# The general path as loops with sums in SBUF, and the branch's flag ahead of the last copies

## The chip, the core and the metric

The kernel runs on one core of one Trainium2 chip. The metric is the time of one execution on the device, in microseconds (us). Engines: PE (TensorE), DVE (VectorE), ACT (ScalarE), POOL (GpSimd) and SP (SyncE); PEld is PE's weight load.

## The reference

A gated linear recurrence, whose output is the input of a feed-forward block:

```python
f = 1.0 / (1.0 + np.exp(-f_logit))
for t in range(S):
    state = f[:, :, t, :, None] * state + np.einsum('bhd,bhe->bhde', k[:, :, t], v[:, :, t])
    y[:, :, t] = np.einsum('bhd,bhde->bhe', q[:, :, t], state)
...
h = x @ w_in
sp = np.where(h > 20.0, h, np.log1p(np.exp(np.minimum(h, 20.0))))
g = h * np.tanh(sp)
return (g @ w_out).astype(np.float32)
```

Batch 4, 8 heads, 768 positions, head size 48; `x` is the recurrence's output as 3072 rows of 384, `w_in` is 384 x 2048 and `w_out` 2048 x 384, all float32.

## The kernel before

The kernel holds two ways to the result and a branch between them.

**The planned path** (lines 240 to 617) does the recurrence in chunks of 128 positions, 24 chunks in all, in a form that divides by running products of `f`, and the feed-forward block in 6 groups of 512 tokens by 16 tiles of d_ff, 96 units in all. A unit is nine matmuls of 128x512 into `h` (`moe_in`, line 212), nine steps of the activation on ACT, DVE and POOL (`mish`, lines 222 to 230), and nine matmuls into the three output banks `o` (`moe_out`, line 235). The activation's two output parts go to PE two units later (`LAG` = 2).

Nothing is issued as it is written. Every step goes to a `Plan` with its engine, an assumed cost and the names that it reads and writes (`add`, line 52). `Plan.order` (line 122) packs all steps forward and backward some fifty times on assumed costs and keeps the packing that ends first; `issue` (line 137) then emits each engine's instructions in that order. So each engine runs a fixed list, and waits between engines are semaphores.

Of the last unit of a group (`out_unit`, line 551), each of the three output tiles m = 0, 1, 2 has a PE step of three matmuls, a copy from PSUM to `ob` (DVE for m = 0 and 2 on line 581, ACT for m = 1 on line 578), and a transfer to `out` that SP issues (line 582).

**The flag.** The planned path's form is good only while the running products stay above a bound. `ends` holds each chunk's last product. Four steps after the loop over units (lines 607 to 613) compare them with the bound on DVE (line 608), add them up per partition on DVE (line 611), over the partitions with a matmul against ones on PE (line 612), and copy the count to `flag` on DVE (line 613).

**The branch.** Line 621 loads `flag` into a register of each engine, and line 622 is a branch of each engine. With this reference's inputs all products are good, so every engine jumps over the body of the branch, the **general path** (lines 623 to 696), which is in the program and doesn't run. Behind the body, each engine brings its semaphores to the counts that the body would have left, and these stand in the trace under line 622. SP has eight of them, for its transfers' semaphores. Then come the waits and the barrier that close the program, under line 758.

The general path is a scan over time per head pair (a loop over batches, the four head pairs written out, a loop over the 48 columns of v for each pair), and then the feed-forward block for a group of 512 tokens at a time (a loop over the six groups, with the 24 gathers of its input and the 16 d_ff tiles written out). So it has six loops in its code. As compiled, the body that the branch jumps over has these numbers of instructions: PE 740, SP 381, ACT 278, DVE 244, POOL 169. SP's 381 are 55 transfers with about 105 instructions for their addresses, and for the rest the loops' scaffolding (branches, barriers, semaphores).

Of the kernel before, what the change touches and what calls it, by code (L numbers as in the profile page):

```python
# [160 lines left out]
def T_DVE(n):  # L161
    return n / 0.96 + 70
# [7 lines left out]
def recurrence_moe_kernel(  # L170
# [34 lines left out]
    state0 = ctile([P, P], F32, "state0")  # L205


    def moe_in(h, xt, j):
        n = 0
        for a in range(NK):  # L210
            for w, x in ((wih, 0), (wih, 1), (wil, 0)):
                nc.tensor.matmul(  # L212
                    h, w[:, j, a * P : (a + 1) * P], xt[:, x, a, :], start=(n == 0), stop=(n == 3 * NK - 1)
                )
                n += 1
# [14 lines left out]
            ("pool", T_POOL(GT), 1, lambda: nc.gpsimd.tensor_tensor(gl, g, gh.bitcast(F32), ALU.subtract)),  # L230
        )

    def moe_out(o, m, gh, gl, j, first, last):
        for i, (w, x) in enumerate(((woh, gh), (wol, gh), (woh, gl))):
            nc.tensor.matmul(  # L235
                o, w[:, j, m * P : (m + 1) * P], x, start=(first and i == 0), stop=(last and i == 2)
            )


    with tc.tile_pool(name="work", bufs=1) as pool, tc.tile_pool(  # L240
# [307 lines left out]
        while done < 4 * GC:  # L548
            attend()

        def out_unit(u):
            g, j = units[u]
            half = g < 2
            first = j == 0 or (half and j == HF)
            last = j == NF - 1 or (half and j == HF - 1)
            part = half and j == NF - 1
            gs = u % 3
            if part:
                for m in range(NK):
                    add("sp", 500, lambda m=m, g=g: nc.sync.dma_start(ob_[m], halves[g][m * P : (m + 1) * P, :]),  # L560
                        [("half", g, m)], pairs(("ob", m)), 262)
            if u == 0:
                plan.until = len(plan.steps)
            if last or first:
                for m in range(NK):
                    add("pe", 702, lambda m=m: moe_out(o_[m], m, gh_[gs], gl_[gs], j, first, last),
                        [("w", "h", j), ("w", "l", j), ("gh", gs), ("gl", gs)], [("o", m)])
            else:
                add("pe", 2106, lambda: [moe_out(o_[m], m, gh_[gs], gl_[gs], j, first, last) for m in range(NK)],
                    [("w", "h", j), ("w", "l", j), ("gh", gs), ("gl", gs)], [("o", m) for m in range(NK)])  # L570
            if last:
                dst = halves[g] if j < NF - 1 else out[:, g * GT : (g + 1) * GT]
                for m in range(NK):
                    if part:
                        add("dve", T_DVE(GT), lambda m=m: nc.vector.tensor_tensor(ob_[m], o_[m], ob_[m], ALU.add),
                            [("o", m)], pairs(("ob", m)))
                    elif m == 1:
                        add("act", T_ACT(GT, True), lambda m=m: nc.scalar.activation(ob_[m], o_[m], AF.Copy),  # L578
                            [("o", m)], pairs(("ob", m)))
                    else:  # L580
                        add("dve", T_DVE(GT), lambda m=m: nc.vector.tensor_copy(ob_[m], o_[m]), [("o", m)], pairs(("ob", m)))
                    add("sp", 500, lambda m=m, dst=dst: nc.sync.dma_start(dst[m * P : (m + 1) * P, :], ob_[m]),
                        pairs(("ob", m)), [("half", g, m) if half else ("out", g, m)], 262)

        for u in range(len(units) + LAG):
            if u < len(units):
                g, j = units[u]
                if g == 0:
                    split_w(j)
                x, hs, us, gs = g % 2, u % 2, u % 2, u % 3  # L590
                xk = [(hl, ("xt", x, c), p) for hl in "hl" for c in range(GC) for p in range(NK)]
                h = h_[hs]
                add("pe", 2106, lambda h=h, x=x, j=j: moe_in(h, xt_[x], j), xk + [("w", "h", j), ("w", "l", j)], [("h", hs)])
                kh, kn, kg = ("h", hs), ("n", us), ("g", us)
                ops = mish(h, n_[us], g_[us], gh_[gs], gl_[gs])
                rw = (
                    ([kh], [kn]), ([], [kn]), ([], [kn]), ([kh, kn], [kg]), ([kn], [kh]), ([], [kh]),
                    ([kh], [kg]), ([kg], [("gh", gs)]), ([kg, ("gh", gs)], [("gl", gs)]),
                )
                for (e, c, shared, fn), (r, w) in zip(ops, rw):  # L600
                    add(e, c, fn, r, w, port=shared)
            while done < min(4 * NCH, attend_goal(u)):
                attend()
            if u >= LAG:
                out_unit(u - LAG)

        ok, oks = at1[0:1, 0:1], state.rearrange("p b a c -> p (b a c)")[:, : NCH * NP]
        add("dve", 119, lambda: nc.vector.tensor_scalar(
            oks, ends.rearrange("p n a b -> p (n a b)"), -DEC_OK, None, ALU.is_le),
            [x for n in range(NCH) for x in pairs(("end", n))], [("st", b) for b in range(B)])  # L610
        add("dve", 169, lambda: nc.vector.tensor_reduce(okc, oks, mybir.AxisListType.X, ALU.add), [("st", 0)], ["okc"])
        add("pe", 26, lambda: nc.tensor.matmul(ok, ones, okc, start=True, stop=True), ["okc"], [("at", 2)])
        add("dve", 65, lambda: nc.vector.tensor_copy(flag, ok), [("at", 2)], ["flag"])

        plan.idle = idle
        with tc.manual_schedule():
# [3 lines left out]
    total = P * NCH * NP  # L620
    good = nc.values_load(flag[0:1, 0:1], min_val=0, max_val=total)
    with tc.If(good < total):
        xs = dram.tile([DM, NT], F32, tag="xs", name="xs")
        with tc.tile_pool(name="slow", bufs=1) as pool, tc.tile_pool(
            name="slow_psum", bufs=1, space=PSUM
# [6 lines left out]
            nc.gpsimd.memset(sel[0:64, 0:1], 1.0)  # L632
            nc.gpsimd.memset(sel[64:128, 1:2], 1.0)
            with tc.For_i(0, B, 1) as b:
                for p in range(NP):
                    f, k, q = (st([P, NCB, C], nm) for nm in ("sf", "sk", "sq"))
                    for dst, src in ((f, fl), (k, kk), (q, qq)):
                        nc.sync.dma_start(
                            dst, src.rearrange("(c b) p a t -> p a c b t", b=B)[:, p, :, ds(b, 1), :]
                            .rearrange("p c b t -> p c (b t)"),  # L640
                        )
                    nc.scalar.activation(f, f, AF.Sigmoid)
                    f2, k2, q2 = (x.rearrange("p c t -> p (c t)") for x in (f, k, q))
                    with tc.For_i(0, D, 1) as e:
                        v = st([P, S], "sv")
                        for i in range(2):
                            nc.sync.dma_start(
                                v[64 * i : 64 * i + 64, :],
                                vt[ds(b, 1), 2 * p + i, ds(e, 1), :]
                                .rearrange("a c t -> (a c) t")  # L650
                                .broadcast_to([64, S]),
                            )
                        nc.vector.tensor_tensor(v, v, k2, ALU.mult)
# [8 lines left out]
                            nc.scalar.activation(y[:, s], ps, AF.Copy)  # L662
                        for i in range(2):
                            nc.sync.dma_start(
                                xs.rearrange("d (c b t) -> d c b t", b=B, t=C)[ds(e + (2 * p + i) * D, 1), :, ds(b, 1), :]
                                .rearrange("d c b t -> d (c b) t"),
                                y[i : i + 1, :].rearrange("d (c t) -> d c t", c=NCB),
                            )

            with tc.For_i(0, NG, 1) as g:  # L670
                x = st([P, NK, GT], "sx")
                tok = ds(g * GT, GT)
                for a in range(NK):
                    for e in range(2):
                        r, hd = 64 * e, head_at(a, e)
                        for m in range(3):
                            nc.sync.dma_start(
                                x[r + m : r + 64 : 4, a, :], xs[hd * D + m : (hd + 1) * D : 3, tok]
                            )
                        r0 = head_at(NP - 1, e) * D  # L680
                        nc.sync.dma_start(x[r + 3 : r + 64 : 4, a, :], xs[r0 + a : r0 + D : 3, tok])
                xt = pool.tile([P, 2, NK, GT], F32R, tag="sxt", name="sxt")
                nc.scalar.activation(xt[:, 0], x, AF.Copy)
                nc.vector.tensor_tensor(xt[:, 1], x, xt[:, 0].bitcast(F32), ALU.subtract)
                h, *o = (psum.tile([P, GT], F32, tag=f"so{m}", name=f"so{m}") for m in range(NK + 1))
                n, g = (st([P, GT], nm) for nm in ("sn", "sg"))
                gh, gl = (pool.tile([P, GT], F32R, tag=nm, name=nm) for nm in ("sgh", "sgl"))
                for j in range(NF):
                    moe_in(h, xt, j)
                    for *_, step in mish(h, n, g, gh, gl):  # L690
                        step()
                    for m in range(NK):
                        moe_out(o[m], m, gh, gl, j, j == 0, j == NF - 1)
                for m in range(NK):
                    nc.vector.tensor_copy(g, o[m])
                    nc.sync.dma_start(out[m * P : (m + 1) * P, tok], g)


_SHAPES = [
# [63 lines left out]
```

## Time and profile before

| what | us |
|---|---|
| median of three runs (534.45 to 538.31) | 536.96 |
| the profiled execution, its own time | 537.24 |
| its span, from the first to the last instruction | 535.5 |
| outside the span (537.24 less 535.5) | 1.7 |

The profile shows busy times of engines; instructions that only wait, branch, load a register or issue a transfer belong to an engine's sequencer, are marked with a q behind the engine's name, and are not busy time.

### The profile page before, as it was taken

The numbers are of one execution on the slowest core, as the hardware profiler recorded it, in microseconds if no ns is written. First come the engines' busy times: TensorE is split into PE (matmuls) and PEld (weight loads), VectorE is DVE, ScalarE is ACT, GpSimd is POOL, SyncE is SP. The second block draws the span as 40 slices with busy tenths as digits, with TensorE's granted clock in tenths as the row PEclk, the third lists the DMA queues.
The fourth block names the chain that finished last, engine by engine and source line by source line (L and its number), as shares of the span: only waits on it lengthen the run. The fifth ranks groups of instructions, "written<-read, shape, count | busy, mean of one in ns | idle before, by whom it ended". The sixth has DMA issues, their size and how long they took to land.

```text
span 535.5 us, 13156 instructions
## 1 busy us (share of the span) xinstructions
PE 512.4 (96%) x5362; PEld 408.3 (76%) x5362; DVE 382.8 (71%) x617; ACT 415.5 (78%) x746; POOL 174.2 (33%) x153
## 2 busy tenths in 40 slices
PE   7899989899998999999999999999999999999992
PEld 7787767677777777787877777787787778788881
DVE  5988999999996878785767577747565763645441
ACT  7767877799878878878887878878788776777770
POOL 2311332233234434333443333333241322132330
PEclk9999999999999999999999999999999999999997
DMA  7876444424520443231213232202221000100001
GB/s 232 283 242 234 147 138 144 151 87 156 169 74 2 140 139 110 65 115 41 61 40 109 59 102 80 60 21 89 66 94 41 2 1 31 38 21 2 1 1 66
DMA packets 23926, 48.92 MB, mean 91 GB/s; under 512 B 2800, under 2 KB 6256, under 8 KB 23856
## 3 DMA queue, kind: packets, MB, share of 16 engines
q1 hardware_dynamic: 23856, 47.98, 28.1%
q8 instruction: 44, 0.72, 0.5%
q14 instruction: 26, 0.21, 0.1%
HBM read 39.32 MB, written 6.29 MB: 85 GB/s over the span
## 4 chain that ended last, share of the span: by engine, by line
PE 68%; DVE 16%; ACT 6%; DMA 4%; issue 4%; SPq 0%; DVEq 0%; ACTq 0%
PE h L212 31%; PE o L235 29%; DVE n L224 3%; DMA l<-fl 2%; DVE g L225 2%; DVE g L228 2%; PE at L427 2%; DVE wl L324 2%; PE at L462 2%; PE at L474 2%; DVE wt L319 2%; PE at L385 1%; DVE wt L321 1%; DMA xt<-xt 1%; PE at L410 1%
## 5 line engine op out<-in xcount | busy, mean ns | idle before, releaser
L230 POOL TENSOR_TENSOR gl<-g,gh 128x512 fp32r<-128x512 f32 x96 | 128.3, 1337 | 265.9 <-ACT gh L229 247.6
L212 PE MATMUL h<-xt,wh 128*128 128x512 f32 x576 | 185.2, 402 | 8.4 <-DVE g L228 5.3
L212 PEld LDWEIGHTS h<-xt,wh 128*128 128x128 f32 x576 | 104.6, 188 | 37.0 <-DVE g L228 9.2
L235 PE MATMUL o<-gh,wh 128*128 128x512 f32 x288 | 116.0, 403 | 0.0
L212 PE MATMUL h<-xt,wl 128*128 128x512 f32 x288 | 114.1, 396 | 0.1
L235 PE MATMUL o<-gl,wh 128*128 128x512 f32 x288 | 114.1, 396 | 0.0
L235 PE MATMUL o<-gh,wl 128*128 128x512 f32 x288 | 113.3, 393 | 0.0
L224 DVE SCALAR_TENSOR_TENSOR n<-n 128x512 f32<-128x512 f32 x96 | 70.7, 737 | 57.6 <-ACT n L223 57.5
L228 DVE TENSOR_TENSOR g<-g,h 128x512 f32<-128x512 f32 x96 | 65.2, 681 | 40.1 <-ACT h L227 39.7
L222 ACT ACTIVATE n<-h,hcap 128x512 f32<-128x512 f32 x96 | 65.7, 685 | 34.1 <-PE h L212 33.5
L226 ACT ACTIVATE h<-n,two 128x512 f32<-128x512 f32 x96 | 66.0, 688 | 22.7 <-DVE g L225 22.6
L229 ACT ACTIVATE gh<-g 128x512 fp32r<-128x512 f32 x96 | 60.3, 628 | 24.4 <-DVE g L228 22.2
L225 DVE TENSOR_TENSOR g<-h,n 128x512 f32<-128x512 f32 x96 | 66.0, 687 | 7.3 <-POOL gl L230 1.1
L223 ACT ACTIVATE n<-n,hcap 128x512 f32<-128x512 f32 x96 | 69.1, 720 | 2.0
L235 PEld LDWEIGHTS o<-gl,wh 128*128 128x128 f32 x288 | 54.1, 188 | 13.7 <-POOL gl L230 0.6
L212 PEld LDWEIGHTS h<-xt,wl 128*128 128x128 f32 x288 | 54.1, 188 | 13.7 <-DVE wl L324 0.5
L235 PEld LDWEIGHTS o<-gh,wh 128*128 128x128 f32 x288 | 54.1, 188 | 12.8 <-ACT ob L578 0.3
L235 PEld LDWEIGHTS o<-gh,wl 128*128 128x128 f32 x288 | 54.1, 188 | 12.4
L227 ACT ACTIVATE h<-h 128x512 f32<-128x512 f32 x96 | 55.9, 582 | 1.6
L273 POOL TENSOR_TENSOR k<-k,inv 128x512 f32<-128x512 f32 (+1 forms) x26 | 31.7, 1222 | 68.6 <-DVE inv L354 45.4
L354 DVE TENSOR_TENSOR_SCAN inv<-gate,ones 128x516 f32<-128x516 f32 (+1 forms) x28 | 31.7, 1132 | 3.4 <-ACT gate L352 3.4
L304 PE MATMUL o<-state 128*128 128x128 f32 x200 | 28.3, 297 | 1.1 <-DVE gate L288 1.1
(97 smaller groups left out, 517.1 us busy)
## 6 DMA issues: line engine op xcount, KB each, us to landing
raw<-ww SPq DMA_DIRECT2D x16, 768.0 KB, 4.7
v<-vn SPq DMA_DIRECT2D x24, 256.0 KB, 3.9
l<-fl SPq DMA_DIRECT2D x20, 256.0 KB, 2.7
k<-kk SPq DMA_DIRECT2D x20, 256.0 KB, 2.9
q<-qq SPq DMA_DIRECT2D x20, 256.0 KB, 3.3
out<-ob SPq DMA_DIRECT2D x18, 256.0 KB, 2.1
xt<-xt SPq DMA_DIRECT2D x15, 128.0 KB, 2.5
half<-ob SPq DMA_DIRECT2D x6, 256.0 KB, 2.3
```

Of the source, the lines that this page charges most:

```text
L212: nc.tensor.matmul(h, w[:, j, a * P : (a + 1) * P], xt[:, x, a, :], start=(n == 0), stop=(n == 3 * NK - 1))
L222: ("act", T_ACT(GT, True, 1), 0, lambda: nc.scalar.activation(u, h, AF.Relu, bias=hcap, scale=-1.0)),
L223: ("act", T_ACT(GT, False, 1), 0, lambda: nc.scalar.activation(u, u, AF.Exp, bias=hcap, scale=-1.0)),
L224: ("dve", T_DVE(GT), 1, lambda: nc.vector.scalar_tensor_tensor(n, u, 2.0, u, ALU.add, ALU.mult)),
L225: ("dve", T_DVE(GT), 0, lambda: nc.vector.tensor_tensor(g, h, n, ALU.mult)),
L226: ("act", T_ACT(GT, False, 1), 0, lambda: nc.scalar.activation(h, n, AF.Ln, bias=two)),
L227: ("act", T_ACT(GT, True), 0, lambda: nc.scalar.activation(h, h, AF.Exp, scale=-1.0)),
L228: ("dve", T_DVE(GT), 0, lambda: nc.vector.tensor_tensor(g, g, h, ALU.mult)),
L229: ("act", T_ACT(GT), 0, lambda: nc.scalar.activation(gh, g, AF.Copy)),
L230: ("pool", T_POOL(GT), 1, lambda: nc.gpsimd.tensor_tensor(gl, g, gh.bitcast(F32), ALU.subtract)),
L235: nc.tensor.matmul(o, w[:, j, m * P : (m + 1) * P], x, start=(first and i == 0), stop=(last and i == 2))
L273: add("pool" if on_pool else "dve", cost, lambda: eng.tensor_tensor(dst, x, y, ALU.mult), reads, writes, port=port)
```

## The change

The four steps of the flag become a function, `check`, which is called ahead of the second to last unit's output part; the DVE copies of the very last unit (m = 0 and m = 2) read `flag`, so they come behind it. The steps themselves are the same.

In the general path the four head pairs become a loop, the three row tiles of the input a loop (their gathers, eight an iteration, are issued by ACT in place of SP), and the sixteen d_ff tiles a loop. An iteration of that loop copies its weight tiles to two buffers, does its matmuls with start and stop on each, and adds its output to a sum in SBUF, which is what is written out. The general path then has six loops in its code again: over batches, pairs, columns, groups, row tiles and d_ff tiles.

```diff
+        def check():
+            ok, oks = at1[0:1, 0:1], state.rearrange("p b a c -> p (b a c)")[:, : NCH * NP]
+            add("dve", 119, lambda: nc.vector.tensor_scalar(
+                oks, ends.rearrange("p n a b -> p (n a b)"), -DEC_OK, None, ALU.is_le),
+                [x for n in range(NCH) for x in pairs(("end", n))], [("st", b) for b in range(B)])
+            add("dve", 169, lambda: nc.vector.tensor_reduce(okc, oks, mybir.AxisListType.X, ALU.add), [("st", 0)], ["okc"])
+            add("pe", 26, lambda: nc.tensor.matmul(ok, ones, okc, start=True, stop=True), ["okc"], [("at", 2)])
+            add("dve", 65, lambda: nc.vector.tensor_copy(flag, ok), [("at", 2)], ["flag"])
...
-                        add("dve", T_DVE(GT), lambda m=m: nc.vector.tensor_copy(ob_[m], o_[m]), [("o", m)], pairs(("ob", m)))
+                        add("dve", T_DVE(GT), lambda m=m: nc.vector.tensor_copy(ob_[m], o_[m]),
+                            [("o", m)] + ["flag"] * (u == len(units) - 1), pairs(("ob", m)))
...
+            if u == len(units):
+                check()
             if u >= LAG:
                 out_unit(u - LAG)
-
-        ok, oks = at1[0:1, 0:1], state.rearrange("p b a c -> p (b a c)")[:, : NCH * NP]
...
             with tc.For_i(0, B, 1) as b:
-                for p in range(NP):
+                with tc.For_i(0, NP, 1) as p:
...
-                for a in range(NK):
+                rows = xs.rearrange("(a e r m) t -> a e m r t", e=2, r=D // 3, m=3)
+                with tc.For_i(0, NK, 1) as a:
                     for e in range(2):
...
+                        for m in range(4):
+                            src = rows[ds(a, 1), e, m, :, tok] if m < 3 else rows[NP - 1, e, ds(a, 1), :, tok]
+                            nc.scalar.dma_start(
+                                x[64 * e + m : 64 * e + 64 : 4, ds(a, 1), :], src.rearrange("a r t -> r a t")
                             )
...
-                for j in range(NF):
-                    moe_in(h, xt, j)
-                    for *_, step in mish(h, n, g, gh, gl):
+                with tc.For_i(0, NF, 1) as j:
+                    for w, whole in zip(wj, (wh, wl)):
+                        nc.vector.tensor_copy(w, whole[:, ds(j, 1), :].bitcast(F32))
+                    moe_in(h, xt, 0, *(w[:, :, : NK * P] for w in wj))
+                    for *_, step in mish(h, n, g_, gh, gl):
                         step()
                     for m in range(NK):
-                        moe_out(o[m], m, gh, gl, j, j == 0, j == NF - 1)
+                        moe_out(o[m], m, gh, gl, 0, True, True, *(w[:, :, NK * P :] for w in wj))
+                        nc.vector.tensor_tensor(total_o[:, m], total_o[:, m], o[m], ALU.add)
```

`moe_in` and `moe_out` take the weight views as arguments, with the old ones as defaults.

## Rows read from the trace of the kernel before

**Rows 1.** The page: busy time of the engines, PE's share in 40 slices.
```profile
PE 512.4 (96%) x5362; PEld 408.3 (76%) x5362; DVE 382.8 (71%) x617; ACT 415.5 (78%) x746; POOL 174.2 (33%) x153
...
PE   7899989899998999999999999999999999999992
```
**Rows 2.** The stretch behind the last copy: length, busy us of each engine (count).
```profile
526.30:535.50 9.20, 0.00 (x0) 0.00 (x0) 0.00 (x0) 0.00 (x0) 0.00 (x0) 0.63 0.20 70
```
**Rows 3.** Chain of work that ended last, its end: start us, us, what.
```profile
514.98 10.52 PE o L235 x45
...
525.52 0.69 DVE ob L581
526.21 0.05 DVE flag L613
```
**Rows 4.** Timeline, 523.9 to 526.4: start us, us, instruction, idle before it.
```profile
524.12 0.69 DVE L581 COPY ob<-o 128x512 f32<-128x512 f32 x1 [3.59 <-PE o L235]
...
524.84 1.74 SPq L582 DMA_DIRECT2D out<-ob  x3
...
525.09 0.40 PE L235 MATMUL o<-gl,wh 128*128 128x512 f32 x1
...
525.41 0.19 PE L612 MATMUL at<-okc,ones 128*1 128x1 f32 x2
```
**Rows 5.** Line 621: SP's load of the flag (ns, start us).
```profile
L621 SPq TENSOR_LOAD <-flag x1: 508/508/508, 526.6 to 526.6; - x1
```
**Rows 6.** Line 622: branches, and first instructions behind them (ns, starts us).
```profile
L622 POOLq COMPARE_BRANCH  x1: 45/45/45, 527.1 to 527.1; - x1
L622 DVEq COMPARE_BRANCH  x1: 72/72/72, 527.2 to 527.2; - x1
L622 PEldq COMPARE_BRANCH  x1: 3682/3682/3682, 527.2 to 527.2; - x1
L622 SPq COMPARE_BRANCH  x1: 50/50/50, 527.5 to 527.5; - x1
L622 POOLq EVENT_SEMAPHORE  x1: 17/17/17, 527.6 to 527.6; - x1
...
L622 DVEq EVENT_SEMAPHORE  x1: 21/21/21, 531.1 to 531.1; - x1
```
**Rows 7.** Lines 622 and 758: SP's closing list, in three stretches.
```profile
L622 SPq EVENT_SEMAPHORE  x7: 17/17/17, 531.2 to 531.7; - x7
...
L622 SPq EVENT_SEMAPHORE  x1: 17/17/17, 533.7 to 533.7; - x1
...
L758 SPq EVENT_SEMAPHORE  x8: 28/28/28, 533.8 to 534.2; - x8
...
L758 SPq EVENT_SEMAPHORE  x2: 17/17/17, 534.8 to 535.4; - x2
```
**Rows 8.** DMA queues (packets, MB): whole run, then 527.6 to 529, 531.8 to 533.
```profile
q8 instruction: 44, 0.72, 0.5%
q14 instruction: 26, 0.21, 0.1%
...
q14 instruction: 4, 0.03, 7.8%
...
q14 instruction: 2, 0.02, 3.2%
```
**Rows 9.** Line 611: the flag's sum on DVE.
```profile
L611 DVE TENSOR_REDUCE okc<-state x1: 254/254/254, 445.6 to 445.6; 128x1 f32<-128x96 f32 x1
```
**Rows 10.** Timeline of PE: from large matmuls to small ones.
```profile
314.08 0.39 PE L235 MATMUL o<-gh,wl 128*128 128x512 f32 x1
314.31 0.40 PE L235 MATMUL o<-gl,wh 128*128 128x512 f32 x1
314.63 0.69 PE L427 MATMUL at<-v,kt 64*64 64x64 f32 x32
```
**Rows 11.** Waits of PE, the largest: us in total, times, longest us.
```profile
PE h L212 <- DVE g L228: 5.3, 7, 2.0
```

More of the change, by code (lines that the diff above doesn't have):

```diff
@@ L205, in recurrence_moe_kernel, with moe_in @@
     state0 = ctile([P, P], F32, "state0")
-    def moe_in(h, xt, j):
+    def moe_in(h, xt, j, wih=wih, wil=wil):
         n = 0
@@ L231, in mish, with moe_out @@
         )
-    def moe_out(o, m, gh, gl, j, first, last):
+    def moe_out(o, m, gh, gl, j, first, last, woh=woh, wol=wol):
         for i, (w, x) in enumerate(((woh, gh), (wol, gh), (woh, gl))):
@@ L603, in recurrence_moe_kernel @@
                 attend()
+            if u == len(units):
+                check()
             if u >= LAG:
                 out_unit(u - LAG)
-        ok, oks = at1[0:1, 0:1], state.rearrange("p b a c -> p (b a c)")[:, : NCH * NP]
[L608 to L613, printed above, removed]
         plan.idle = idle
@@ L638, in recurrence_moe_kernel @@
                         nc.sync.dma_start(
-                            dst, src.rearrange("(c b) p a t -> p a c b t", b=B)[:, p, :, ds(b, 1), :]
-                            .rearrange("p c b t -> p c (b t)"),
+                            dst, src.rearrange("(c b) p a t -> p a c b t", b=B)[:, ds(p, 1), :, ds(b, 1), :]
+                            .rearrange("p a c b t -> p (a c) (b t)"),
                         )
@@ L648, in recurrence_moe_kernel @@
                                 v[64 * i : 64 * i + 64, :],
-                                vt[ds(b, 1), 2 * p + i, ds(e, 1), :]
-                                .rearrange("a c t -> (a c) t")
+                                vt.rearrange("b (p i) e s -> b p i e s", i=2)[ds(b, 1), ds(p, 1), i, ds(e, 1), :]
+                                .rearrange("a p c t -> (a p c) t")
                                 .broadcast_to([64, S]),
@@ L664, in recurrence_moe_kernel @@
                             nc.sync.dma_start(
-                                xs.rearrange("d (c b t) -> d c b t", b=B, t=C)[ds(e + (2 * p + i) * D, 1), :, ds(b, 1), :]
-                                .rearrange("d c b t -> d (c b) t"),
+                                xs.rearrange("(i p d) (c b t) -> i p d c b t", i=2, d=D, b=B, t=C)[
+                                    i, ds(p, 1), ds(e, 1), :, ds(b, 1), :
+                                ].rearrange("p d c b t -> (p d b) c t"),
                                 y[i : i + 1, :].rearrange("d (c t) -> d c t", c=NCB),
@@ L672, in recurrence_moe_kernel @@
                 tok = ds(g * GT, GT)
-                for a in range(NK):
+                rows = xs.rearrange("(a e r m) t -> a e m r t", e=2, r=D // 3, m=3)
+                with tc.For_i(0, NK, 1) as a:
                     for e in range(2):
[L675 to L678, printed above, removed]
-                            )
-                        r0 = head_at(NP - 1, e) * D
-                        nc.sync.dma_start(x[r + 3 : r + 64 : 4, a, :], xs[r0 + a : r0 + D : 3, tok])
+                        for m in range(4):
+                            src = rows[ds(a, 1), e, m, :, tok] if m < 3 else rows[NP - 1, e, ds(a, 1), :, tok]
+                            nc.scalar.dma_start(
+                                x[64 * e + m : 64 * e + 64 : 4, ds(a, 1), :], src.rearrange("a r t -> r a t")
+                            )
                 xt = pool.tile([P, 2, NK, GT], F32R, tag="sxt", name="sxt")
@@ L685, in recurrence_moe_kernel @@
                 h, *o = (psum.tile([P, GT], F32, tag=f"so{m}", name=f"so{m}") for m in range(NK + 1))
-                n, g = (st([P, GT], nm) for nm in ("sn", "sg"))
+                n, g_ = (st([P, GT], nm) for nm in ("sn", "sg"))
                 gh, gl = (pool.tile([P, GT], F32R, tag=nm, name=nm) for nm in ("sgh", "sgl"))
-                for j in range(NF):
-                    moe_in(h, xt, j)
-                    for *_, step in mish(h, n, g, gh, gl):
+                wj = [pool.tile([P, 1, W_TILE], F32R, tag=nm, name=nm) for nm in ("swh", "swl")]
+                total_o = st([P, NK, GT], "so")
+                nc.vector.memset(total_o, 0.0)
+                with tc.For_i(0, NF, 1) as j:
[3 more added lines that the diff above has]
+                    for *_, step in mish(h, n, g_, gh, gl):
                         step()
                     for m in range(NK):
-                        moe_out(o[m], m, gh, gl, j, j == 0, j == NF - 1)
+                        moe_out(o[m], m, gh, gl, 0, True, True, *(w[:, :, NK * P :] for w in wj))
+                        nc.vector.tensor_tensor(total_o[:, m], total_o[:, m], o[m], ALU.add)
                 for m in range(NK):
-                    nc.vector.tensor_copy(g, o[m])
-                    nc.sync.dma_start(out[m * P : (m + 1) * P, tok], g)
+                    nc.sync.dma_start(out[m * P : (m + 1) * P, tok], total_o[:, m])
 _SHAPES = [
```

## The prediction

> **What bounds the kernel now.** I read the page first: PE is busy for 512.4 of 535.5 us and at nine tenths or more in nearly all slices [rows 1]. The chain of work that ended last says the same for the end: it is PE's output matmuls without a break up to 525.50, then a copy on DVE and the flag [rows 3]. But it stops at 526.26, and the span lasts until 535.5. The stretch table shows no engine busy in those 9.2 us [rows 2]. So the time has two parts: a PE-bound plan of 526 us, which the change barely touches, and a tail of 9.2 us, 1.7% of the time, in which only sequencers run. The tail has to be read from the lines of the flag's load, the branch and the program's close, since no view of busy time shows it.
>
> SP is last in the tail. It issues the third output transfer when the last copy is done (its three issues end at 526.58 [rows 4]), loads the flag from 526.6 [rows 5], and branches at 527.5 [rows 6]. Its next instruction starts at 531.2, 3.7 us later. It does seven semaphores by 531.7, stops for 2.0 us, does the eighth at 533.7, eight waits until 534.2, and the barrier to the end [rows 7]. The others are at the barrier by then: DVE's first instruction behind its branch is at 531.1, PE's branch takes 3.7 us from 527.2, and POOL alone goes straight on, from 527.1 to 527.6 [rows 6].
>
> The gaps are fetches of code. Between 527.6 and 529 four packets move on the instruction queue of the engines beside PE, and two more between 531.8 and 533, when SP stands still [rows 8]. A packet there is 0.21 MB / 26 = 8 KB, on PE's queue 0.72 MB / 44 = 16 KB [rows 8]; PE's 5,362 matmuls and as many weight loads [rows 1] make its 0.72 MB some 67 bytes an instruction, so I take 64, and 8 KB is 128 instructions. Against the body's lengths this fits: POOL jumps over 169 and has its code at hand, while DVE with 244, SP with 381 and PE with 740 have to fetch.
>
> SP's position follows. It stops after seven instructions, so its jump of 381 lands 7 ahead of a boundary between blocks of code; counted from the branch, boundaries then lie at 388, 260, 132 and 4. The block behind the branch's own reaches to 132, and a longer jump has missed it.
>
> **The general path.** No instruction of it runs, so its new copies, adds and ACT transfers cost nothing; with cover gone there is nothing to pay, as the branch is not entered. What counts is the length of each jump. SP's body has 55 transfers now (four pairs of 7, 24 gathers, 3 outputs) and 10 afterwards (7, none, 3). At (55 + 105) / 55 = 2.9 instructions each, 45 fewer take 131 off 381. The number of loops, six, and with it the scaffolding, stays. So about 250; nested loops and the ACT transfers' semaphores make this uncertain by 25 either way. PE loses 15 of 16 tiles of 18 matmuls, with a weight load each, 540 of 740. DVE, ACT and POOL end near 150, 185 and 135 by the same counting.
>
> SP at 225 to 275 is still beyond 132: it misses, and the 3.7 us stay. The other engines get shorter jumps, and may save their fetch, which is worth nothing: they wait for SP at the barrier (DVE's 531.1 against SP's last wait at 534.2). What can change is the second stop. SP has about 22 instructions in its closing list (8 semaphores, 8 waits, drains, barrier [rows 7]). It stops again if a boundary, at 260, lies 1 to 22 behind the landing, so for jumps of 238 to 259. From 225 to 275 that is 22 of 51 places, 43%. Otherwise the eighth semaphore follows the seventh after (531.7 - 531.2) / 6 = 0.08 us in place of 2.0, a gain of 1.9. I take 1.9, the likelier; the other end is below.
>
> **The flag.** The comparison and the sum ran at 445.6, when DVE had a gap, 80 us ahead of need [rows 9]; they stay there, at nothing (bound: their 0.45 us, were they late). The matmul runs as two passes, now behind the last output matmul: 525.09, 525.41 and 0.19 us for both [rows 4]. There it costs PE nothing that matters, since DVE is still copying. Moved ahead of a copy, it has to stand between output matmuls, where PE is the bound. Those start 0.23 us apart; from a large one to a small one it is 0.32 [rows 10], as at 525.09 to 525.41. That is 0.09 more, 0.03 to the second pass, and up to 0.16 until the next large one starts: 0.12 to 0.28. I take 0.27, as the next weight load has no large matmul to hide under.
>
> The new wait is that of two DVE copies for the flag. Behind them on DVE is nothing else; SP's transfers wait for them. Before the m = 0 copy DVE sits idle for 3.59 us [rows 4], which hides the flag's 0.13 us; so nothing. Without that cover (the matmul ahead of the last three alone) the m = 2 copy is about 0.3 us late; with the matmul still last both copies follow, and it is 1.1.
>
> What leaves the end is the flag's own copy, 0.05 us beyond the last copy [rows 3]. It is worth nothing either: the loads of the other engines start earlier, but SP's load starts when its third transfer is issued, and that waits for the last copy, not for the flag. What is late next is what was late before, SP. Bounds: 0 to 0.05 gained.
>
> **The sum.** 537.24 - 1.9 + 0.27 = 535.6 us by the profiled execution. The median of the runs is 0.28 lower, so 535.3.
>
> [...] For fetches the rows say: packets of 8 KB, and a jump of 244 stalls DVE where one of 169 didn't stall POOL [rows 6, 8]. [...]
>
> **The cases.**
> A, the forecast: SP still fetches behind its branch and doesn't stop a second time. 535.3.
>
> B: the landing again lies 1 to 22 ahead of a boundary, so the second stop stays, shorter or longer. The pause ends 2.5 us after the landing (531.2 to 533.7); compared with a stop after 7, one after 1 ends 0.5 us later and one after 22 about 1.0 earlier. With PE's 0.27: 536.2 to 537.7, say 537.0. For it speaks the count of 250, 10 ahead of the boundary; against it only the spread of the count.
>
> C: SP has its code at hand, as POOL had. Then it goes on at 528.0 in place of 531.2, and without the second stop: 3.2 + 1.9 - 0.27 = 4.8 less, 532.1. The last output's 2 us of transfer from 526.2 end before SP asks for it. Against it: 250 is nearer to DVE's 244 than to POOL's 169, and the boundary at 132.
>
> D, slower: SP's closing list grows. ACT's queue is new, and if its transfers carry semaphores of their own, SP may have up to eight more to level at 0.08 us and eight more to wait for at 0.06 [rows 7]: 1.1 us. The list is then 38 long and holds a boundary more often, so that the second stop stays. With PE's 0.27: 538.3. It decides from the point where the list is longer than what the lost stop saves. The flag's copies queued behind a late matmul (1.1 us) would add to the same side.
>
> E: the planner packs anew, and one changed order runs through the plan. PE's longest single wait now is 2.0 us, and all its waits of that kind are 5.3 [rows 11]; PE has 535.5 - 9.2 - 512.4 = 13.9 us idle ahead of the tail, so no order gains more. I take 2 us either way. Against it: the flag's steps hang on nothing else in the plan, and only the last two copies hang on them.
>
> **How the numbers follow.** A 0.50, B 0.31, C 0.06, D 0.06, E 0.07. A measurement of this kernel can tell about 1% (5.4 us) from no change, as its three runs lie within 0.7%. Only a C with luck or a large E gets below 531.6: 0.05. Above 542.3 takes an E beyond its 2 us: 0.03. The rest, 0.92, is within 1%. The range holds A and B with the spread of runs, and half of E, and leaves out C and D, at 0.12 together: 533.0 to 538.1.
>
> **What would show it.** Right: PE's tiny matmul stands between the output matmuls near 523 us and the flag's copy ahead of the last DVE copy; SP's branch is again followed by a gap of 3 to 4 us, and its semaphores of lines 622 and 758 then run without a stop of 2 us; the other engines' gaps behind the branch shrink to about 0.4. B shows as a stop of 1 to 2.5 us at another place of that list, C as SP's first semaphore at 528, D as more than eight SP semaphores under line 622. Wrong altogether: a change of more than 2 us ahead of 526 us, where the plan runs.

## The result and the profile after

The kernel after took 532.88 us (median of 8 runs, 531.15 to 534.57), the kernel before 537.13 beside it (median of 8). The ratio is 0.9925 with a 95% interval of 0.9898 to 0.9952, that is by the ratio 4.0 us less (2.6 to 5.5). The forecast was 1.6 us less, so the direction held and the size was too small; the median lies 0.1 us under the low end of the range.

The profiled execution's span fell from 535.5 to 529.4 us, by 6.1. Not all of that is the change. PE's busy time by stretches, in the kernel before and the one after (columns: stretch, its length, busy us of PE, PEld, DVE, ACT and POOL with counts, granted clock, DMA share, GB/s):

```profile
0.00:137.00 137.00, 125.49 (x1683) 102.16 (x1684) 123.38 (x200) 110.25 (x217) 39.92 (x45) 1.00 0.55 180
137.00:445.00 308.00, 306.27 (x3335) 241.90 (x3335) 221.03 (x359) 247.56 (x439) 109.77 (x89) 1.00 0.23 72
```
```profile
0.00:137.00 137.00, 129.53 (x1695) 105.31 (x1696) 127.38 (x204) 113.00 (x222) 41.61 (x46) 0.99 0.57 185
137.00:445.00 308.00, 306.29 (x3337) 242.28 (x3336) 219.53 (x358) 246.99 (x439) 108.53 (x88) 1.00 0.23 71
```

In the first 137 us PE got 4 us more done, afterwards the same. The DVE instruction that starts at 137.27 in the trace before starts at 134.28 after. Nothing of the change runs there, and in the 14 traces of this study that instruction starts anywhere from 133.9 to 143.5, also among kernels that differ only behind the branch. So these 3.0 us lie within what single executions differ by, and I take them as the luck of one. From that instruction's start to the start of the last DVE copy it takes 388.2 us before and 388.5 after. What is left is the tail, from the end of the last copy to the end of the span: 9.26 us before, 5.94 after.

The flag's matmul, copy and SP's load in the kernel after (timeline of PE and DVE, then line 626):

```profile
463.83 0.40 PE L235 MATMUL o<-gl,wh 128*128 128x512 f32 x1
...
464.16 0.19 PE L557 MATMUL at<-okc,ones 128*1 128x1 f32 x2
464.28 0.50 PE L235 MATMUL o<-gh,wh 128*128 128x512 f32 x1
...
465.37 0.14 DVE L558 CAST flag<-at 1x1 int32<-1x1 f32 x1
```
```profile
L626 SPq TENSOR_LOAD <-flag x1: 747/747/747, 465.5 to 465.5; - x1
```

The planner put the matmul 59 us ahead of the last copy, not 2. Large matmuls stand 0.45 us apart around it in place of 0.23, so it costs PE 0.22. And SP no longer loads the flag behind its last transfer, as in [rows 5], but at 465.5, as soon as it exists. Then the branch, line 627, and the program's close, line 770 (ns, first and last start us), the close first up to 528.3 and then whole:

```profile
L627 SPq EVENT_SEMAPHORE  x8: 17/17/17, 526.9 to 527.4; - x8
...
L627 PEldq COMPARE_BRANCH  x1: 223/223/223, 520.5 to 520.5; - x1
...
L627 DVEq COMPARE_BRANCH  x1: 72/72/72, 523.6 to 523.6; - x1
L627 SPq COMPARE_BRANCH  x1: 50/50/50, 523.8 to 523.8; - x1
L627 DVEq EVENT_SEMAPHORE  x1: 21/21/21, 524.2 to 524.2; - x1
```
```profile
L770 SPq EVENT_SEMAPHORE  x9: 17/28/28, 527.5 to 528.2; - x9
```
```profile
L770 SPq EVENT_SEMAPHORE  x10: 17/28/28, 527.5 to 529.3; - x10
...
L770 SPq DRAIN  x3: 7/7/116, 528.0 to 529.1; - x3
```

Against [rows 6, 7]: PE's branch takes 0.22 us in place of 3.68, and DVE goes on after 0.6 in place of 3.9. SP still stands still for 3 us behind its branch, from 523.9 to 526.9. Its eight semaphores and eight waits then run without the stop of 2 us, but a stop is there: its last drain starts at 529.1, 0.85 us behind the instruction ahead of it. That is after 19 instructions.

I split the tail at the end of SP's branch and at the start of its next instruction, from the times in the traces (us). Each row is one trace; the last column has the length of SP's jump and the number of instructions behind it after which SP stops:

| kernel | copy to branch | branch to next | to the end | tail | SP's jump, stop after |
|---|---|---|---|---|---|
| before | 1.34 | 3.62 | 4.31 | 9.26 | 381, 7 |
| after | 0.46 | 2.97 | 2.51 | 5.94 | 241, 19 |
| flag alone | 0.46 | 3.47 | 3.88 | 7.82 | 381, 7 |
| general path alone | 1.33 | 3.02 | 2.39 | 6.74 | 241, 19 |
| 12 drains in the body | 0.46 | 2.96 | 3.83 | 7.25 | 254, 6 |
| transfers on ACT | 0.46 | 2.94 | 1.91 | 5.31 | 204, none |
| transfers on ACT, 20 drains ahead | 0.46 | 0.45 | 3.35 | 4.26 | 204, none |
| 12 drains ahead | 0.46 | 0.44 | 3.83 | 4.73 | 241, 7 |
| 24 drains ahead | 0.46 | 2.93 | 1.91 | 5.30 | 241, none |
| DVE and ACT miss | 0.46 | 2.87 | 2.69 | 6.02 | 242, 18 |
| PE misses | 0.46 | 3.09 | 2.49 | 6.03 | 242, 18 |
| PE, DVE and ACT miss | 0.46 | 2.94 | 2.52 | 5.92 | 242, 18 |
| SP's old length | 0.46 | 2.90 | 3.50 | 6.87 | 381, 7 |
| all old lengths | 0.46 | 3.12 | 3.48 | 7.06 | 381, 7 |

The jumps are counted in the compiled programs; with drains in the body the count is one more than the drains add (242 where SP has none). "Ahead" means ahead of the branch, "in the body" in the general path, which doesn't run. "Miss" means that the named engines' jumps are made long again, so that they wait for their code: PE's branch took 3.76 and 3.32 us, and DVE's next instruction started 3.5 and 3.7 us after its branch. A drain is an instruction that is put in here only for the place that it takes in the code.

### The profile page after: what moved, and what is told of

Read it like the earlier page. It is cut to its first block, busy times and chain, and to the rows that moved or that the text cites. A ratio compares the mean times of both kernels' runs of the same rounds, so it can differ in the third digit from the quotient of the medians.

```text
span 529.4 us, 13158 instructions
## 1 busy us (share of the span) xinstructions
PE 513.5 (97%) x5362; PEld 409.4 (77%) x5362; DVE 384.0 (73%) x617; ACT 415.2 (78%) x746; POOL 174.7 (33%) x153
## 4 chain that ended last, share of the span: by engine, by line
PE 72%; DVE 13%; ACT 8%; issue 3%; DMA 2%; DVEq 0%; ACTq 0%
PE h L212 32%; PE o L235 30%; DVE n L224 3%; PE at L427 2%; PE at L474 2%; PE at L462 2%; DVE g L225 2%; DVE g L228 2%; PE at L385 2%; DMA l<-fl 2%; DVE wl L324 1%; PE at L410 1%; ACT h L226 1%; DVE wt L321 1%; DVE wt L319 1%
```

## The experiments

**The two halves of the change.** The first has the flag's part of the diff alone, the second the general path's alone.

```diff
+            if u == len(units):
+                check()
```

> The flag ahead of the last copies, with the general path as it was. I measure the tail from the end of the last DVE copy to the end of the span: 9.26 us before, 5.94 after the whole change, in three pieces: to the end of SP's branch 1.34 before and 0.46 after, from there to SP's next instruction 3.6 and 3.0, from there to the end 4.3 and 2.5. Theory: the early flag lets SP load it ahead of its last transfers, so the first piece alone shrinks, to 0.46; the last stays at 4.3 with the stop after seven semaphores, since SP's jump is still 381; the middle is 3.6, or 3.0 if it was long because four engines fetched at once. Tail 7.8 to 8.4. Rival: the flag's place is worth nothing and SP's load stays behind the last transfer: tail 9.2. A second rival has the whole gain from the flag: 5.9.

> The general path as loops, with the flag made last as before. SP's jump is 241, which lands 19 instructions ahead of a block boundary. Theory: first piece 1.34 as before, middle 3.0 to 3.6, last 2.5, as in the whole change, with a stop of 0.7 us after 19 instructions in place of 2.0 after 7. Tail 6.8 to 7.4. Rival: all of the gain is the flag's: tail 9.2, last piece 4.3.

The flag alone: ratio 0.9979 (0.9947 to 1.0012), by itself no clear difference, tail 7.82. The general path alone: 0.9945 (0.9907 to 0.9983), tail 6.74. So the flag gives 0.88 us in the first piece, by SP's load, and takes 0.24 back on PE (from the instruction at 137 us to the last copy it is 388.5 us in every kernel with the early matmul, 388.2 in the two without). The general path gives about 2.5 by its own tail, and 1.9 by the whole change against the flag alone: the flag alone, with the old jump and the old stop, is 0.15 and 0.43 shorter in the second and third pieces than the kernel before. In the first trace PE misses as before and SP stops at the old place; in the second neither does:

```profile
L626 SPq EVENT_SEMAPHORE  x8: 17/17/17, 528.6 to 530.8; - x8
...
L626 PEldq COMPARE_BRANCH  x1: 3702/3702/3702, 521.8 to 521.8; - x1
...
L626 SPq COMPARE_BRANCH  x1: 50/50/50, 525.1 to 525.1; - x1
```
```profile
L624 SPq EVENT_SEMAPHORE  x8: 17/17/17, 531.0 to 531.5; - x8
...
L624 PEldq COMPARE_BRANCH  x1: 223/223/223, 527.6 to 527.6; - x1
```

**Moving the stop.** If SP stops at the end of a block of 128 instructions, the place follows from the length of a body that never runs. The 128 is the estimate from packets of 8 KB and 64 bytes an instruction; in the trace after, 42 packets of 16 KB on q8 for PE's 10,724 matmuls and weight loads make 64 too. The first run makes it longer, the second shorter (all of its transfers on ACT).

```diff
+            for _ in range(12):
+                nc.sync.drain()
             sel = st([P, 2], "sel")
```

> The whole change, with 12 drains more on SP at the head of the general path, which doesn't run: SP's jump is 254 and lands 6 ahead of the boundary. Theory: six semaphores, then a stop of about 2 us, so the last piece is 4.2 to 4.4 and the tail 7.6 to 7.8. Rival: the stop of 2 us was a wait for a transfer or another engine, and the length of a body that isn't run can't bring it back: tail 5.9.

> The whole change, with all transfers of the general path issued by ACT: SP's jump is 204, lands 60 ahead of a boundary. Theory: SP still misses (204 is beyond the 132 that its next block reached, and its branch lies four instructions earlier in its block), so the middle stays at 3.0, and there is no second stop at all: last piece 1.7 to 1.8, tail 5.1 to 5.3. ACT's jump of 210 may miss now, which costs nothing. Rival: the stop after 19 instructions was the barrier's own and stays: tail 5.9. A second rival, that a shorter jump finds its code at hand: middle 0.4, tail 2.6 to 3.5.

With 12 drains the first six semaphores ran from 529.4 to 529.8 and the last two at 531.7, in two stretches of line 627:

```profile
L627 SPq EVENT_SEMAPHORE  x6: 17/17/17, 529.4 to 529.8; - x6
...
L627 SPq EVENT_SEMAPHORE  x2: 17/17/17, 531.7 to 531.8; - x2
```

The stop came after six, as counted; the last piece, 3.83, was 0.4 short of what I expected. With the transfers on ACT there was no stop, 1.91 against 1.7 to 1.8; its ratio to the kernel before is 0.9934 (0.9900 to 0.9968). So the stop is a boundary in SP's code and no wait for a transfer.

**Moving the branch.** Now the same for the first fetch. Drains on SP shift its branch and everything behind it. I had put them near 440 us; in the traces they run between 466 and 470, still 59 us ahead of the branch.

```diff
-                    add("sp", 500, lambda m=m, dst=dst: nc.sync.dma_start(dst[m * P : (m + 1) * P, :], ob_[m]),
+                    add("sp", 500, lambda m=m, dst=dst, g=g: (nc.sync.dma_start(dst[m * P : (m + 1) * P, :], ob_[m]),
+                        [nc.sync.drain() for _ in range(12 * (g == NG - 2 and m == 0))]),
```

> The whole change, SP's jump 241 as there, with 12 drains on SP near 440 us: the branch lies 8 into a block and lands in the next, 7 ahead of its end. Theory of blocks: the same jump now finds its code, middle 0.4 in place of 3.0; it then stops after seven semaphores until the block behind has come, 2.2 to 2.5 us after the landing. Tail 4.7 to 5.2. Rival, that the length alone decides: middle 3.0, tail 5.9.

> The same with 24 drains: the jump of 241 ends 5 instructions beyond the next block. Theory of blocks: a miss again, middle 3.0, and no second stop, as the next boundary is 123 behind: last piece 1.8 to 2.0, tail 5.2 to 5.5. Rival, that drains in front help in some other way: middle 0.4 as with 12.

> The general path's transfers all on ACT (SP's jump 204), and 20 drains on SP near 440 us, where SP is idle, so that SP's branch lies 12 into a block and lands 76 into the next, 40 ahead of its end. Theory: SP reads its code in blocks of 128 and has the next one at hand, so the branch costs 0.4 as on the other engines, and there is no second stop. What is late next is the landing of the last output, 2.9 us behind the last copy, for which SP's seventh semaphore waits. Pieces 0.46, 0.4 and 3.3 to 3.7, tail 4.2 to 4.6, against 5.3 with the same jump and no drains; against the kernel before 4.7 + 0.9 - 0.24 = 4.4 to 4.9 us less, a ratio near 0.991. Rival: a jump of 204 is too long wherever it stands: middle 3.0, tail 5.3.

With 12 drains ahead the jump of 241 took 0.44 us, with 24 it took 2.93 again, and both tails, 4.73 and 5.30, came as the theory of blocks has them. The lines for 12 (the semaphores in two stretches), then 24 (line 628):

```profile
L628 SPq EVENT_SEMAPHORE  x7: 17/17/17, 526.9 to 528.7; - x7
```
```profile
L628 SPq EVENT_SEMAPHORE  x1: 17/17/17, 529.4 to 529.4; - x1
```
```profile
L628 SPq COMPARE_BRANCH  x1: 45/45/45, 526.4 to 526.4; - x1
```
```profile
L628 SPq EVENT_SEMAPHORE  x8: 17/17/17, 531.4 to 532.0; - x8
...
L628 SPq COMPARE_BRANCH  x1: 50/50/50, 528.4 to 528.4; - x1
```

With 12 the sixth and seventh semaphores wait for the last output transfers first, which land at 527.90 and 528.69; the eighth stands 2.4 us behind the first.

So length alone doesn't decide: counted in blocks of 128, the same jump of 241 took 0.44 us where it ends inside the block behind the branch's own, and 2.93 where it ends five instructions beyond.

The third run, with SP's transfers on ACT and 20 drains ahead, has both: 0.45 us behind the branch and no second stop. (It lands 88 instructions into the block, not 76; 40 ahead of the end holds.) It took 531.31 us against 537.66 for the kernel before beside it, ratio 0.9874 (0.9834 to 0.9914), that is 6.8 us less (4.6 to 8.9), of which its tail, 5.00 shorter than before, less PE's 0.24 accounts for 4.8. Beside the whole change it was not run; its tail is 1.68 us shorter than that one's. It is 4.26 us, and another thing ends it:

```profile
L628 SPq EVENT_SEMAPHORE  x7: 17/17/17, 527.8 to 529.7; - x7
...
DMA to landing us min/median/max: 2.0/2.8/2.9
```

The last transfer is issued 0.03 us after the copy and lands 2.8 us later, at 529.68, and SP's seventh semaphore waits for that.

**Why SP's fetch took 3.0 in place of 3.6.** I had not foreseen this 0.65 us. Five tries, with drains in the body on other engines, on SP, or on all (the first one's edit):

```diff
+            for _ in range(140):
+                nc.vector.drain()
+                nc.scalar.drain()
```

> The whole change, with 140 drains on each of DVE and ACT at the head of the general path, which doesn't run: their jumps are 290 and 318, so that they miss as before; SP's is 242. Theory that fetches at the same time delay each other: SP's middle piece goes from 3.0 to between 3.4 and 3.7. Rival, that SP's fetch was faster for its own shorter jump: it stays at 2.9 to 3.0.

> The whole change, with 400 drains on PE at the head of the general path, which doesn't run: PE's jump is 576 and misses, as in the two runs where SP's middle piece was 3.5 and 3.6; the other jumps are short. Theory P, that PE's fetch of a larger block holds up SP's: middle 3.4 to 3.7. Theory S, that it was SP's own longer jump: 2.9 to 3.0.

> The whole change, with 139 drains on SP at the head of the general path: SP's jump is 381 as before the change, lands 7 ahead of a boundary, and no other engine misses. Theory S: middle 3.4 to 3.7. Theory P: 2.9 to 3.0. By both, seven semaphores and a second stop of 1.6 to 2.0; last piece 3.8 to 4.3.

> The whole change, with the drains on PE (400) and on DVE and ACT (140 each) together, so that all three miss as before the change, and SP's jump stays at 242. Theory that several fetches at once delay SP's: middle 3.4 to 3.7, as in the kernel before (3.62) and in the flag alone (3.47), the two runs where all of them missed. Rival, that the 0.6 us comes from something else that no drain brings back (the fetch of 8 KB is of a varying length): 2.9 to 3.1.

> The whole change, with drains at the head of the general path that bring every engine's jump back to its old length: PE 740, SP 381, ACT 278, DVE 244, POOL 169. This is the flag alone as far as the sequencers' positions go, with another body. Theory that the lengths make the middle piece together, if no one of them does: 3.4 to 3.6, last piece 3.8 to 4.3 with a stop after seven semaphores, tail 7.7 to 8.3, as with the flag alone (3.47, 3.88, 7.82). Rival: the 0.5 to 0.6 us hang on something else of the old program: middle 2.9 to 3.1, last piece 3.5 to 4.0, tail 6.9 to 7.5.

Misses on DVE and ACT, on PE, on all three, and SP's old length left it at 2.87, 3.09, 2.94 and 2.90; all old lengths together gave 3.12, still under 3.47 and 3.62. My theory of fetches that delay each other falls for SP. DVE's gap in the first of them is 3.5 us, but that engine isn't last:

```profile
L627 DVEq COMPARE_BRANCH  x1: 72/72/72, 525.3 to 525.3; - x1
L627 SPq COMPARE_BRANCH  x1: 50/50/50, 525.4 to 525.4; - x1
...
L627 DVEq EVENT_SEMAPHORE  x1: 21/21/21, 528.8 to 528.8; - x1
```

The two longer ones belong to the two programs with the old general path, one trace each. Whether something in it costs SP about half a microsecond, and what, stays open.

The last piece shows the same. With SP's old length it is 3.50 and with all old lengths 3.48, under the 3.88 of the flag alone and the 4.31 of the kernel before, though SP stops after seven in all four. The semaphores with SP's old length, then with all:

```profile
L627 SPq EVENT_SEMAPHORE  x8: 17/17/17, 531.1 to 533.2; - x8
```
```profile
L627 SPq EVENT_SEMAPHORE  x8: 17/17/17, 530.1 to 532.2; - x8
```

The eighth follows the first after 2.1 us in both, as with the flag alone, and after 2.55 in the trace before. And in the two programs with the old path the barrier is 0.37 us longer than in these two runs: POOL's first and second semaphore there are 0.38 us apart, in all others 0.07. Why, no run shows.

## Why the prediction was right, and where it wasn't

**The frame was right.** From 137 us on the plan takes as long as before, up to a quarter of a microsecond, and the change acts in the tail, through the fetches of code and the flag's load. The 3.0 us ahead of that would by themselves have met the sign for "wrong altogether"; they come and go between executions of the same plan. In the tails' account: 0.88 in the first piece, 0.65 in the second, 1.80 in the third, less 0.24 on PE, is 3.1 us, inside the measured 2.6 to 5.5. The forecast's 1.9 - 0.27 = 1.6 is not.

**The jump and the second stop.** The count of about 250 for SP's jump came out at 241, inside the 238 to 259 for which I had said that the stop returns. So by its condition case B held, not A: SP stops again, after 19. By its price it was nearly A: 1.80 in place of 1.9. What was mis-sized is B's price. I let the instructions behind the boundary cost 0.07 us each; but the barrier is among them, and most of its 1.1 us now passes ahead of the stop's end. The stop also ends 2.2 us behind the landing, not 2.5. That 1.80 came so near to 1.9 is in part luck: without any second stop the last piece is 1.91, which is 2.4 less, and SP's old length brings back only 1.0 of the 1.80. Of the other 0.8, 0.4 is that the stop in the trace before ended later, and 0.4 is its longer barrier; the reason of both stays open.

**The flag.** The step that failed is "what leaves the end is worth nothing", with its bounds of 0 to 0.05 us. I took SP's load to stay where it stood, behind the third transfer. It went to where the flag is ready, 58 us earlier, and the 0.88 us of load and register instructions between the last transfer and the branch left SP's path: from the end of the copy to the end of the branch it is 0.46 in place of 1.34, with the flag alone as with the whole change. An order in the queue that came from the data was read as a fixed one.

PE's price was right: 0.27 forecast, 0.22 by the gap between the matmuls and 0.24 over the whole stretch. The matmul's place was not: 464 us, not near 523. The copies' wait costs nothing, as said; the flag is there 56 us before the first of them.

**The branch's fetch** I had at 3.7 on both sides; it fell to 3.0, in every kernel with the new path and a miss. Those 0.65 us are the other part that was missing, and their cause stays open. That the other engines' shorter jumps are worth nothing is borne out: with PE, DVE and ACT missing again, the tail was 5.92 against 5.94.

**Rivals.** C did not come, but the run with 12 drains ahead shows how near it was: it took twelve more instructions ahead of the branch. Its price left out that the last output would then be waited for: in the run with 20 drains ahead that lands 2.8 us after its issue, and SP's seventh semaphore stands behind it. D did not come: line 627 has eight SP semaphores as before. E neither: between 137 us and the last copy all traces with the early flag agree within 0.06 us.

## What to carry to other kernels

Behind the last busy instruction look at the sequencers: in these traces a branch over code that never runs kept SP for 2.87 to 3.62 us in twelve of them and for 0.44 and 0.45 in two, and a second stop took up to 2.0 us more. Which of these was paid fits a count of branch and landing in blocks of 128 instructions, and twelve drains ahead of the branch were enough to go from 2.97 us to 0.44, twelve more to go back to 2.93. Make a branch's condition early enough that the register load leaves the last engine's path (0.88 us here), and look at that engine's whole queue, since the load can go ahead of its transfers (58 us here). And compare stretches before spans: here half of the 6.1 us between two profiles was the start of one execution.

## What the runs showed of the hardware

SP's jump of 241 took 0.44 us with 12 drains ahead of its branch, 2.97 with none and 2.93 with 24. Where SP stopped a second time, it went on 2.1 to 2.5 us after the landing. In the trace after, two packets moved on q14 in SP's gap from 523.9 to 526.9 us and one between 526.9 and 529.1, ahead of the end of its second stop. A packet of code was 8 KB on q14, the queue that I take for the engines beside PE, and 16 KB on q8, which I take for PE's: one moved on it between 527.2 and 531.2 us in the trace before, when PE's branch took 3.68, and none from 520 to 529.1 in the trace after, when it took 0.22. One and the same DVE instruction started at 133.9 to 143.5 us in 14 executions whose engines' orders are the same up to there, which the medians have to carry.
